# A two-layer decode kernel: V in natural 4 KB runs, exponent on turned scores, one pool of 27 halves, and every K and V load issued as two of 64 partitions

## The chip, the cores and the metric

The kernel runs on one core of a Trainium2 chip. The core has TensorE (PE, matmuls; PEld is its weight load), VectorE (DVE), ScalarE (ACT), GpSimd (POOL) and SyncE (SP, here the only engine that issues transfers), a memory of 128 partitions beside them, and 16 DMA engines that bring data from the large memory. The metric is the device time in microseconds (us), lower is better. The kernel before takes 326.1 us, the median of three runs (323.88 to 326.27).

## The reference

Four tokens, one for each sequence, go twice through an attention block and a feed-forward block; weights and caches are the same both times. Inputs are bfloat16.

```python
# x [4, 1, 448]; k_cache, v_cache [4, 8, 8192, 256]; wq [448, 4096]; wo [4096, 448]
def A(x, k_cache, v_cache, wq, wo):
    W = 2048                                  # min(4096, max(256, 8192 // 4))
    q = (x @ wq).reshape(4, 1, 16, 256).transpose(0, 2, 1, 3)
    k = repeat(k_cache[:, :, 8192 - W:, :], 2, axis=1)   # two query heads to each of 8 K/V heads
    v = repeat(v_cache[:, :, 8192 - W:, :], 2, axis=1)
    p = softmax(einsum("bhqd,bhkd->bhqk", q, k) * 256 ** -0.5)
    o = einsum("bhqk,bhkd->bhqd", p, v)
    return o.transpose(0, 2, 1, 3).reshape(4, 1, 4096) @ wo

def B(x, w_gate, w_up, w_down):               # 448 -> 1792 -> 448
    return (silu(x @ w_gate) * (x @ w_up)) @ w_down

for _ in range(2):
    x = x + A(layernorm(x), k_cache, v_cache, wq, wo)
    x = x + B(layernorm(x), w_gate, w_up, w_down)
```

For one token and one K/V head the last 2048 rows of K and of V are 1 MB each. There are 32 such pairs of token and head, each used in both layers.

## The kernel before

**Work.** The unit is a pair: one token, one layer, one K/V head with its two query heads; there are 64. `steps` lays them out in an order in which token t's first layer runs side by side with token t-1's second layer, shifted by three heads (`SHIFT`), so that the feed-forward block and the next queries of one token are worked out while another token's heads are under way. Of the eight heads of a token five are kept on the chip from the first layer to the second (`KEEP_K`, `KEEP_V`); the other three are loaded twice. So 44 pairs load, and each loads two halves of K and two of V, 512 KB a half.

**A pair** (`pair`, lines 600 to 712). K is loaded in halves in which partition p holds rows 16p to 16p+15, eight of them to a half: one run of 4 KB for each partition (L609). VectorE turns each half in blocks of 32 by 32 into a buffer `KT` (L617), of which there are six, each for a whole K head. GpSimd spreads the queries with a mask (`qe`, L641), so that 32 matmuls (L637) give the scores of all 2048 rows for two query heads in a tile of 128 by 32. VectorE takes the largest of each row (L646), PE spreads it over the partitions (L649), VectorE makes the negated maximum of each query head (L652), and ScalarE the exponents, once for each query head, 128 by 16 (L656). A matmul with a permutation (`permb`, L660) brings the exponents into the order of V's rows, one with ones gives their sums (L663), ScalarE copies them out (`pT`, L666). V is loaded in halves in another order of rows (`(a q g)`), two runs of 2 KB for each partition (L626). Sixteen matmuls multiply with V (L677). The result goes through ScalarE (L689), VectorE (L691), two matmuls (L697) and a multiplication by the inverse sum (L702), which GpSimd works out as a power (L687). `out_proj` multiplies with wo (L724), `residual`, `norm`, `ffn` (L514, L542), `norm` and `qproj` (L473) follow when a token's eight heads are done.

**Buffers.** Fifteen halves (`half`) take all loads of K and V. A half of K is free again after its turn, one of V after its matmuls, or after the second layer's where it is kept. `KT` buffers go round in program order, five of them held for kept heads.

**Order.** Each operation is entered in a graph with an engine, an assumed duration and a rank. `schedule` runs through the graph with an assumed time for every engine and for the DMA channel (`chan`, with `DSTART`, `LAND` and a cost by run length), takes at each moment the waiting operation of lowest rank, and so fixes the order on every engine and the buffer of every load. `_place_waits` then sets the semaphore waits, and `emit` writes the program. SyncE issues the loads in the order found and waits, before each, for the operation that freed its buffer. `KLEAD` and `VLAG` put K's loads 2.2 pairs ahead of their pair and V's 1.3 behind in rank.

Of the kernel before, what the change touches and what calls it, by code (L numbers as in the profile page):

```python
# [6 lines left out]
ALU = mybir.AluOpType  # L7
# [6 lines left out]
B = 4  # L14
# [11 lines left out]
NKT = 6  # L26
NPOOL = 15
# [7 lines left out]
SLEAD = 1.5  # L35
# [8 lines left out]
LAND = 1.5  # L44
DSTART = 2.1
# [10 lines left out]
class Op:  # L56
    __slots__ = ("i", "eng", "dur", "rank", "emit", "deps", "succ", "nbytes", "dsem", "dval",
                 "start", "end", "pos", "waits", "inc", "val", "known", "run", "cell", "rel")

    def __init__(self, i, eng, dur, rank, emit):  # L60
# [7 lines left out]
        self.rel = ()  # L68
        self.inc = False
# [4 lines left out]
class Graph:  # L74
# [12 lines left out]
    def op(self, eng, dur, rank, emit, r=(), w=(), bank=(), acc=()):  # L87

        o = Op(len(self.ops), eng, dur, rank, emit)
        self.ops.append(o)  # L90
# [23 lines left out]
    def dma(self, rank, nbytes, emit, sem, r=(), w=(), run=8192, cell=None):  # L114

        o = self.op(SP, 0.05, rank, emit, r=r, w=w)
        o.run = run
        o.nbytes = nbytes
        o.cell = cell
        if cell is None:  # L120
            self._count(o, sem)
        return o

    def _count(self, o, sem):
        o.dsem = sem
        self.dcount[sem] = self.dcount.get(sem, 0) + 16
        o.dval = self.dcount[sem]


    def schedule(self, npool):  # L130
# [11 lines left out]
        chan = 1.0  # L142
# [3 lines left out]
        while n < len(self.ops):  # L146
            best = None
            for e, lst in avail.items():
                if not lst:
                    continue  # L150
                t = max(free[e], min(ready_at[o] for o in lst))
                if e == SP:
                    first = min((o for o in lst if ready_at[o] <= t + 1e-9), key=lambda o: (o.rank, o.i))
                    if first.cell is not None:
                        if not pool:
                            continue
                        t = max(t, min(pool)[0])
                if best is None or t < best[0]:
                    best = (t, e)
            assert best is not None, "the graph does not complete"  # L160
            t, e = best
            o = min((o for o in avail[e] if ready_at[o] <= t + 1e-9), key=lambda o: (o.rank, o.i))
            if o.cell is not None:
# [4 lines left out]
                self._count(o, f"h{slot[1]}")  # L168
# [4 lines left out]
            free[e] = t + o.dur  # L173
            o.end = t + o.dur
            if o.nbytes:
                chan = max(chan, t + DSTART) + o.nbytes / 16 * (0.007 / o.run + 1 / 26.6e3)
                o.end = chan + LAND - TAIL[SP]
# [50 lines left out]
    def emit(self, eng_name, eng, sems, dsems):  # L228
        for o in self.order[eng_name]:
# [6 lines left out]
            if o.dsem is not None:  # L236
                ins.then_inc(dsems[o.dsem], 16)
# [41 lines left out]
def build(nc, A_x, A_k_cache, A_v_cache, A_wq, A_wo, B_x, B_w_gate, B_w_up, B_w_down, out):  # L279
# [3 lines left out]
    with ExitStack() as es:  # L283
# [9 lines left out]
        KT = [sb(f"KT{s}", [128, 16 * DH], BF16) for s in range(NKT)]  # L293
        identb = sb("identb", [128, 128], BF16)
        permb = sb("permb", [128, 128], BF16)
        onesb = sb("onesb", [128, 128], BF16)
# [526 lines left out]
```

## Time and profile before

| what | value |
|---|---|
| time, median of 3 runs | 326.1 us (323.88 to 326.27) |
| profiled execution, span from the first to the last instruction | 322.9 us |
| mean granted TensorE clock | 1.000 |
| bytes read from the large memory | 104.44 MB, 323 GB/s over the span |
| busy: PE, DVE, ACT, POOL | 232.6, 192.6, 72.4, 84.9 us |
| DMA packets | 42,327, mean 326 GB/s |
| loads of K and of V | 88 each of 512 KB |

The time is that of separate runs; the profile is one execution, of which only the span is known (322.9 us). The page divides the span into 40 slices of about 8.1 us with a digit for the busy tenths of each engine, and names groups of instructions by line and tile. A wait is put down to what ended last. The DMA share is the sum of the times of all packets over the time of 16 engines; it can be a little over 1, where packets of one engine overlap.

### The profile page before, as it was taken

To read this page: it belongs to the slowest core of one execution; us is meant where nothing else is said; L and a number is where in the kernel's file an instruction comes from. 1 tells how busy PE (TensorE), PEld (TensorE's weight loads), DVE (VectorE), ACT (ScalarE), POOL (GpSimd) and SP (SyncE) were. 2 spreads that over 40 slices of the span, in tenths; PEclk is the share of its full clock that TensorE was granted. 3 is DMA by queue.
4 is the path that set the end of the run, shared out by engine and by line. 5 is a ranking of instruction groups with operands and counts; after the bars stand their busy time and mean duration, and the time that the engine had idled before them with its cause. 6 is when DMAs were issued, how large, how long until landed. Compare 5 with 4: busy or idle time off the path is not lost.

```text
span 322.9 us, 12873 instructions
## 1 busy us (share of the span) xinstructions
PE 232.6 (72%) x5728; PEld 169.7 (53%) x5728; DVE 192.6 (60%) x608; ACT 72.4 (22%) x289; POOL 84.9 (26%) x199
## 2 busy tenths in 40 slices
PE   3654454446588788578796895679787959889875
PEld 2542322234476465366664653567555636686554
DVE  5386555652145778765447787855377874656332
ACT  1112111111022333211231322113223322123310
POOL 3312111112023223240233331313233413134221
DMA  7999999999999999999889999999899999748000
GB/s 277 399 407 392 393 396 397 391 396 397 391 362 308 338 368 346 400 362 309 301 272 373 375 351 405 355 365 339 277 359 377 357 386 391 277 140 305 5 0 5
DMA packets 42327, 105.27 MB, mean 326 GB/s; under 512 B 3096, under 2 KB 7200, under 8 KB 41888
## 3 DMA queue, kind: packets, MB, share of 16 engines
q1 hardware_dynamic: 42272, 104.45, 88.0%
q8 instruction: 45, 0.74, 0.9%
q14 instruction: 10, 0.08, 0.1%
HBM read 104.44 MB, written 0.00 MB: 323 GB/s over the span
## 4 chain that ended last, share of the span: by engine, by line
DMA 38%; PE 34%; DVE 12%; SPq 7%; issue 5%; ACT 2%; POOL 0%; DVEq 0%
DMA half<-in_A_k_cache_dram 20%; DMA half<-in_A_v_cache_dram 12%; PE Y L677 11%; PE S L637 8%; DVE KT L617 6%; DMA wd_sb<-in_B_w_down_dram 5%; PE Z L473 4%; SPq L389 4%; PE A L724 3%; PE Z L514 3%; DVE oh L691 2%; PE Z L542 2%; SPq L609 2%; DVE small L652 2%; SPq L626 1%
## 5 line engine op out<-in xcount | busy, mean ns | idle before, releaser
L617 DVE STREAM_TRANSPOSE KT<-half 128x1024 uint32<-128x1024 uint32 x88 | 108.3, 1233 | 13.3 <-DMA half<-in_A_k_cache_dram 12.9
L637 PE MATMUL S<-qe,KT 128*128 128x8 bf16 x2048 | 64.6, 168 | 22.4 <-DVE KT L617 18.5
L677 PE MATMUL Y<-half,pT 128*4 128x256 bf16 x1024 | 70.0, 403 | 9.6 <-DMA half<-in_A_v_cache_dram 8.7
L637 PEld LDWEIGHTS S<-qe,KT 128*128 128x128 bf16 x2048 | 59.7, 104 | 30.7 <-DVE KT L617 20.8
L687 POOL TENSOR_TENSOR small<-small 128x2 f32<-128x2 f32 x64 | 44.3, 696 | 113.5 <-DVE small L669 103.3
L656 ACT ACTIVATE praw<-S,small 128x16 bf16<-128x16 f32 x128 | 28.7, 279 | 84.6 <-DVE small L652 83.9
L691 DVE SCALAR_TENSOR_TENSOR oh<-oh,small,Y 128x256 bf16<-128x256 bf16 x64 | 30.1, 472 | 23.9 <-ACT oh L689 23.4
L689 ACT ACTIVATE oh<-Y 128x256 bf16<-128x256 f32 x64 | 24.6, 384 | 74.2 <-PE Y L677 74.2
L641 POOL TENSOR_TENSOR qe<-qc,qmask 128x64 bf16<-128x64 bf16 x64 | 18.6, 294 | 71.3 <-PE S L637 52.3
L677 PEld LDWEIGHTS Y<-half,pT 128*4 128x4 bf16 x1024 | 20.0, 94 | 21.8 <-DMA half<-in_A_v_cache_dram 11.5
L646 DVE TRANSPOSE_TENSOR_REDUCE pmax<-S 128x1 bf16<-128x32 f32 x64 | 13.4, 211 | 27.1 <-PE S L637 25.3
L724 PE MATMUL A<-oT,wo_sb 128*128 128x1 bf16 (+1 forms) x688 | 24.8, 166 | 6.4 <-DVE oT L702 6.1
L724 PEld LDWEIGHTS A<-oT,wo_sb 128*128 128x128 bf16 x688 | 22.2, 105 | 10.5 <-DVE oT L702 8.5
L697 PE MATMUL Y<-osel,oh 128*128 128x2 bf16 x128 | 13.3, 173 | 17.4 <-DVE oh L691 17.2
L652 DVE TENSOR_REDUCE small<-S 128x2 f32<-128x128 f32 x64 | 17.4, 282 | 10.4 <-PE S L649 8.3
L666 ACT ACTIVATE pT<-Y 128x64 bf16<-128x64 f32 x64 | 14.1, 222 | 40.7 <-PE Y L663 40.4
L697 PEld LDWEIGHTS Y<-osel,oh 128*128 128x128 bf16 x128 | 8.8, 111 | 27.0 <-DVE oh L691 24.5
L649 PE MATMUL S<-identb,pmax 128*128 128x128 bf16 x64 | 16.6, 284 | 4.5 <-DVE pmax L646 3.6
L473 PE MATMUL Z<-xn,wq_sb 128*128 128x1 bf16 (+1 forms) x480 | 15.6, 165 | 2.6 <-DMA wq_sb<-in_A_wq_dram 1.9
L473 PEld LDWEIGHTS Z<-xn,wq_sb 128*128 128x128 bf16 x480 | 14.3, 104 | 3.4 <-DMA wq_sb<-in_A_wq_dram 2.0
L669 DVE TENSOR_REDUCE small<-Y 128x2 f32<-128x32 f32 x64 | 11.0, 177 | 7.1 <-ACT pT L666 6.8
L440 POOL TENSOR_SCALAR st<-st 128x1 f32<-128x1 f32 x16 | 4.3, 267 | 41.2 <-DVE st L428 40.7
(76 smaller groups left out, 212.0 us busy)
## 6 DMA issues: line engine op xcount, KB each, us to landing
half<-in_A_k_cache_dram SPq DMA_DIRECT2D x88, 512.0 KB, 7.0
half<-in_A_v_cache_dram SPq DMA_DIRECT2D x88, 512.0 KB, 6.7
wo_sb<-in_A_wo_dram SPq DMA_DIRECT2D x8, 448.0 KB, 12.3
wq_sb<-in_A_wq_dram SPq DMA_DIRECT2D x3, 1024.0 KB, 6.9
wd_sb<-in_B_w_down_dram SPq DMA_DIRECT2D x1, 1568.0 KB, 16.3
wg_sb<-in_B_w_gate_dram SPq DMA_DIRECT2D x1, 1344.0 KB, 14.2
wu_sb<-in_B_w_up_dram SPq DMA_DIRECT2D x1, 1344.0 KB, 14.7
wq_sb<-in_A_wq_dram SPq DMA_DIRECT2D x1, 512.0 KB, 10.4
```

The costliest lines, as they stand in the source:

```text
L473: last = e.matmul(o, lhsT=lhsT, rhs=rhs, start=(cc == 0 and hh == 0 and ee == 0), stop=(cc == 3), skip_group_check=True)
L617: return e.transpose(dst[:, 2 * hf + q * n:2 * hf + q * n + n], src[:, q * n:q * n + n])
L637: last = e.matmul(Sb[s_][:, 8 * gg:8 * gg + 8], lhsT=kt[:, gg, ce // 2, ce % 2, :], rhs=qe[q_][:, ce, :, :], start=(gg == 0 and ce == 0), ...
L641: g.op(POOL, 0.25, pos - SLEAD - 1, lambda e: e.tensor_tensor(qe[q_][:, :, :, :], qc[t][:, kvh, :, :].unsqueeze(2).broadcast_to([128, 8, 4 ...
L652: g.op(DVE, 0.2, pos, lambda e: e.tensor_reduce(negm[s_][:, :], Sb[s_][:, 128:256].rearrange("p (k n) -> p n k", n=2), AX.X, ALU.max, nega ...
L656: g.op(SCA, 0.17, pos, lambda e, n=n: e.activation(praw[s_][:, :].rearrange("p (k n) -> p n k", n=2)[:, n, :], Sb[s_][:, 0:32].rearrange(" ...
L677: last = e.matmul(Yb[p_][32 * gg:32 * gg + 4, 256:512], lhsT=pT[p_][:, 4 * gg + 2 * hv + a, :, :].rearrange("p y n -> p (y n)"), rhs=half[ ...
L687: g.op(POOL, 0.25, pos, lambda e: e.tensor_tensor(ri[p_][:, :], rs[p_][:, :], expo[:, 1:3], op=ALU.pow), r=(f"rs{p_}", "expo"), w=(f"ri{p_ ...
L689: g.op(SCA, 0.28, pos, lambda e: e.activation(oh[p_][:, :], Yb[p_][:, 256:512], ACT.Copy), r=(f"y{p_}",), w=(f"oh{p_}",), bank=(f"Y{p_}",))
L691: g.op(DVE, 0.4, pos, lambda e: e.scalar_tensor_tensor(out=oh[p_][:, :], in0=oh[p_][:, :], scalar=lomask[:, 0:1], in1=Yb[p_][:, 256:512], ...
L697: last = e.matmul(Yb[p_][:, 2 * dh:2 * dh + 2], lhsT=oh[p_][:, :].rearrange("p (m e) -> p e m", e=2)[:, dh, :], rhs=osel[:, :], start=Fals ...
L724: last = e.matmul(Av[:, cc, sl], lhsT=wo_sb[:, 4 * kvh + k, c0:c0 + 128], rhs=oT[si % 2][:, k % 2, k // 2, 0:n], start=False, stop=False, ...
```

## The change

1. V is loaded as K is: partition p holds rows 16p to 16p+15, in halves of eight rows, one run of 4 KB for each partition.
2. The exponent is taken of turned scores. VectorE turns the tile of scores (128 by 32) in blocks of 32 by 32 into `sM`, and adds a mask that leaves each row in one of four column blocks and puts -1e30 into the others; one exponent over 128 by 128 follows, and one matmul with `fold` brings the result into the order of V's rows. The spread maximum gets -1e30 where a partition's parity belongs to the other query head, by one more matmul (`pbig`) behind the scores. The sums are taken from `pT`. The permutation goes.
3. The six `KT` buffers go; turned K takes halves of the same pool, which now has 27, one for each half of K. A half of turned K is free again after its 16 matmuls. The scores are entered as two operations, one for each half. `schedule` gives out buffers to VectorE's turns too, and SyncE leaves three free for them (`RESERVE`).
4. The plan's constants: a shorter `DSTART` and `LAND`, 0.45 us for each issue on SyncE where 0.05 stood, another cost by run length, and a model of the pages in which PE's instructions are fetched. `SLEAD` goes from 1.5 to 1.0.
5. Every K and V load is issued as two, of partitions 0 to 63 and 64 to 127, both counted on the half's semaphore.
6. Some small tiles share memory: `xio` with `oh`, `t1` with `th`, `xb` with `xn`.

The diff, cut to its core:

```diff
-NKT = 6
-NPOOL = 15
+NPOOL = 27
...
-SLEAD = 1.5
+SLEAD = 1.0
...
-LAND = 1.5
-DSTART = 2.1
+RESERVE = 3
+LAND = 0.45
+DSTART = 1.6
+PAGE, PAGE0 = 128, 85
+FETCH0, FETCH1 = 3.7, 4.4
...
-        o = self.op(SP, 0.05, rank, emit, r=r, w=w)
-        o.run = run
+    def dma(self, rank, nbytes, emit, sem, r=(), w=(), run=8192, cell=None, parts=1):
+
+        o = self.op(SP, 0.45 * parts, rank, emit, r=r, w=w, cell=cell)
+        o.run, o.parts = run, parts
...
-        self.dcount[sem] = self.dcount.get(sem, 0) + 16
+        self.dcount[sem] = self.dcount.get(sem, 0) + 16 * o.parts
...
+                spare = len(pool) > (RESERVE if e == SP else 0)
                 if e == SP:
...
+                    if o.cell is not None:
+                        if not spare:
                             continue
                         t = max(t, min(pool)[0])
...
-                chan = max(chan, t + DSTART) + o.nbytes / 16 * (0.007 / o.run + 1 / 26.6e3)
-                o.end = chan + LAND - TAIL[SP]
+                if t + DSTART > chan:
+                    chan, lag = t + DSTART, 0.0
+                chan += o.nbytes / 16 * (0.009 / o.run + 1 / 27.2e3)
+                o.end = chan + LAND + lag - TAIL[SP]
...
-                ins.then_inc(dsems[o.dsem], 16)
+                for i in ins if o.parts > 1 else (ins,):
+                    i.then_inc(dsems[o.dsem], 16)
...
+        iw = identb[:, :].rearrange("p (u a n) -> p u a n", a=4, n=2)
+        g.op(DVE, 0.2, R0, lambda e: e.tensor_reduce(
+            fold[:, :, :], iw.rearrange("p u a n -> p u n a"), AX.X, ALU.max), r=("identb",), w=("fold",))
+        g.op(DVE, 0.2, R0, lambda e: e.tensor_reduce(
+            amask[:, :], iw.rearrange("p u a n -> p a u n"), AX.XY, ALU.max), r=("identb",), w=("amask",))
+        g.op(DVE, 0.1, R0, lambda e: e.tensor_scalar(
+            amask[:, :], amask[:, :], -1.0, BIG, op0=ALU.add, op1=ALU.mult), r=("amask",), w=("amask",))
...
+            npar[:, :], identb[:, :].rearrange("p (y n) -> p n y", n=2), AX.X, ALU.max), r=("identb",), w=("npar",))
+        g.op(DVE, 0.2, R0, lambda e: e.tensor_scalar(
+            pbig[:, :], npar[:, :], -1.0, BIG, op0=ALU.add, op1=ALU.mult), r=("npar",), w=("pbig",))
...
+            def rows(src, hf):
+                v = src[t, kvh, s0:s0 + WIN, :].rearrange("(p j) d -> p (j d)", p=128)
+                return v[:, 2048 * hf:2048 * hf + 2048]
+
+            if (t, kvh) in k_held:
+                ks, kn = k_held.pop((t, kvh))
+            else:
+                ks, kn = [[], []], kk
+                for hf in range(2):
+                    raw = []
+                    g.dma(pos - KLEAD, 1 << 19, lambda e, raw=raw, hf=hf: [e.dma_start(
+                        half[raw[0]][c:c + 64, :], rows(A_k_cache, hf)[c:c + 64, :]) for c in (0, 64)],
+                        None, w=(f"k{kk}_{hf}",), run=4096, cell=raw, parts=2)
+
+                    def tr(e, raw=raw, hf=hf):
+                        src = half[raw[0]][:, :].bitcast(UINT32).rearrange("p (x k s) -> p x k s", x=4, k=8)
+                        dst = half[ks[hf][0]][:, :].bitcast(UINT32).rearrange("p (k x r) -> p x k r", k=8, x=4)
+                        return e.transpose(dst, src)
+                    g.op(DVE, 1.16, pos, tr, r=(f"k{kk}_{hf}",), w=(f"kt{kk}_{hf}",), cell=ks[hf], rel=(raw,))
+            if (t, kvh) in v_held:
+                vs, vn = v_held.pop((t, kvh))
+            else:
+                vs, vn = [[], []], kk
+                for hv in range(2):
+                    g.dma(pos + VLAG, 1 << 19, lambda e, hv=hv: [e.dma_start(
+                        half[vs[hv][0]][c:c + 64, :], rows(A_v_cache, hv)[c:c + 64, :]) for c in (0, 64)],
+                        None, w=(f"v{kk}_{hv}",), run=4096, cell=vs[hv], parts=2)
+
...
-            g.op(PE, 32 * MM, pos - SLEAD, scores, r=tuple(f"kt{ks}_{hf}_{q}" for hf in range(2) for q in range(TRP)) + (f"qe{q_}",), w=(f"s{s_}",), bank=(f"S{s_}",))
+
+            def scores(e, hf):
+                last = None
+                kt = half[ks[hf][0]][:, :].rearrange("p (g c m v) -> p g c v m", g=2, c=4, v=2)
+                for gg in range(2):
+                    for ce in range(8):
+                        last = e.matmul(Sb[s_][:, 16 * hf + 8 * gg:16 * hf + 8 * gg + 8], lhsT=kt[:, gg, ce // 2, ce % 2, :],
+                                        rhs=qe[q_][:, ce, :, :], start=(hf == 0 and gg == 0 and ce == 0),
+                                        stop=(hf == 1 and gg == 1 and ce == 7), skip_group_check=True)
+                if hf == 1:
+                    last = e.matmul(Sb[s_][:, 128:256], lhsT=identb[:, :], rhs=pbig[:, :].unsqueeze(1).broadcast_to([128, 64, 2]), start=True, stop=False,
+                                    skip_group_check=True)
+                return last
+            for hf in range(2):
+                g.op(PE, (16 + hf) * MM + 0.05 * hf, pos - SLEAD, lambda e, hf=hf: scores(e, hf),
+                     r=(f"kt{kn}_{hf}", f"qe{q_}") + (("identb", "pbig") if hf else ()),
+                     bank=(f"S{s_}",), rel=() if keep_k else (ks[hf],), mm=16 + hf, **(dict(acc=(f"s{s_}",)) if hf else dict(w=(f"s{s_}",))))
...
-            g.op(PE, 0.1, pos, lambda e: e.matmul(
-                Sb[s_][:, 128:256], lhsT=pmax[s_][:, 0:1].broadcast_to([128, 128]), rhs=identb[:, :], start=True, stop=True,
-                skip_group_check=True), r=(f"pmax{s_}", "identb"), w=(f"m{s_}",), bank=(f"S{s_}",))
+            g.op(PE, 0.06, pos, lambda e: e.matmul(
+                Sb[s_][:, 128:256], lhsT=pmax[s_][:, 0:1].broadcast_to([128, 128]), rhs=identb[:, :], start=False, stop=True,
+                skip_group_check=True), r=(f"pmax{s_}", "identb"), w=(f"m{s_}",), bank=(f"S{s_}",), mm=1)
+            g.op(DVE, 0.12, pos, lambda e: e.transpose(sM[s_][:, 3, :], Sb[s_][:, 0:32]), r=(f"s{s_}",), w=("sM",),
+                 bank=(f"S{s_}",))
+            g.op(DVE, 0.19, pos, lambda e: e.tensor_tensor(
+                sM[s_][:, :, :], sM[s_][:, 3, :].unsqueeze(1).broadcast_to([128, 4, 32]),
+                amask[:, :].unsqueeze(2).broadcast_to([128, 4, 32]), op=ALU.add), r=("sM", "amask"), w=("sM",))
             g.op(DVE, 0.2, pos, lambda e: e.tensor_reduce(
-                negm[s_][:, :], Sb[s_][:, 128:256].rearrange("p (k n) -> p n k", n=2), AX.X, ALU.max, negate=True),
+                negm[s_], Sb[s_][:, 128:256], AX.X, ALU.max, negate=True),
                 r=(f"m{s_}",), w=(f"negm{s_}",), bank=(f"S{s_}",))
-            for n in range(2):
-                g.op(SCA, 0.17, pos, lambda e, n=n: e.activation(
-                    praw[s_][:, :].rearrange("p (k n) -> p n k", n=2)[:, n, :],
-                    Sb[s_][:, 0:32].rearrange("p (k n) -> p n k", n=2)[:, n, :], ACT.Exp, bias=negm[s_][:, n:n + 1]),
-                    r=(f"s{s_}", f"negm{s_}"), w=(f"praw{s_}_{n}",), bank=(f"S{s_}",))
-            g.op(PE, 0.03, pos, lambda e: e.matmul(Yb[p_][:, 64:96], lhsT=permb[:, :], rhs=praw[s_][:, :], start=True,
-                                                   stop=False, skip_group_check=True),
-                 r=(f"praw{s_}_0", f"praw{s_}_1", "permb"), w=(f"yp{p_}",), bank=(f"Y{p_}",))
-            g.op(PE, 0.03, pos, lambda e: e.matmul(Yb[p_][:, 32:64], lhsT=onesb[:, :], rhs=praw[s_][:, :], start=False,
-                                                   stop=False, skip_group_check=True),
-                 r=(f"praw{s_}_0", f"praw{s_}_1", "onesb"), w=(f"ysum{p_}",), bank=(f"Y{p_}",))
-            g.op(SCA, 0.13, pos, lambda e: e.activation(
-                pT[p_][:, :, :, :], Yb[p_][:, 64:96].rearrange("p (k n) -> p k n", n=2).unsqueeze(2).broadcast_to(
-                    [128, 16, 2, 2]), ACT.Copy), r=(f"yp{p_}",), w=(f"pT{p_}",), bank=(f"Y{p_}",))
+            g.op(SCA, 0.26, pos, lambda e: e.activation(
+                praw[s_][:, :], sM[s_][:, :, :].rearrange("p a r -> p (a r)"), ACT.Exp, bias=negm[s_]),
+                r=("sM", f"negm{s_}"), w=(f"praw{s_}",))
+            g.op(PE, 0.05, pos, lambda e: e.matmul(
+                Yb[p_][:, 0:32], lhsT=praw[s_][:, :], rhs=fold[:, :, :], start=True, stop=True, skip_group_check=True),
+                r=(f"praw{s_}", "fold"), w=(f"yp{p_}",), bank=(f"Y{p_}",), mm=1)
+            g.op(SCA, 0.15, pos, lambda e: e.activation(
+                pT[p_][:, :, :, :], Yb[p_][:, 0:32].rearrange("p (u n) -> p u n", n=2).unsqueeze(2).broadcast_to(
+                    [128, 16, 2, 2]), ACT.Copy),
+                r=(f"yp{p_}",), w=(f"pT{p_}",), bank=(f"Y{p_}",))
+            g.op(PE, 0.03, pos, lambda e: e.matmul(
+                Yb[p_][:, 32:64], lhsT=onesb[:, 0:1].broadcast_to([128, 128]), rhs=pT[p_][:, :, 0, :], start=False, stop=False, skip_group_check=True),
+                r=(f"pT{p_}", "onesb"), w=(f"ysum{p_}",), bank=(f"Y{p_}",), mm=1)
...
-                for a in range(2):
-                    for gg in range(4):
-                        last = e.matmul(Yb[p_][32 * gg:32 * gg + 4, 256:512],
-                                        lhsT=pT[p_][:, 4 * gg + 2 * hv + a, :, :].rearrange("p y n -> p (y n)"),
-                                        rhs=half[vs[hv][0]][:, 1024 * a + 256 * gg:1024 * a + 256 * gg + 256], start=False, stop=False, skip_group_check=True)
+                for jj in range(8):
+                    u = 4 * (jj // 2) + 2 * hv + jj % 2
+                    gg = jj % 4
+                    last = e.matmul(Yb[p_][32 * gg:32 * gg + 4, 256:512],
+                                    lhsT=pT[p_][:, u, :, :].rearrange("p y n -> p (y n)"),
+                                    rhs=half[vs[hv][0]][:, 256 * jj:256 * jj + 256], start=False, stop=False,
+                                    skip_group_check=True)
                 return last
             for hv in range(2):
...
+                g.op(PE, 0.53, pos, lambda e, hv=hv: pv(e, hv), r=(f"pT{p_}", f"v{vn}_{hv}"), bank=(f"Y{p_}",),
+                     rel=() if keep_v else (vs[hv],), mm=8, **(dict(acc=(f"y{p_}",)) if hv else dict(w=(f"y{p_}",))))
...
```

More of the change, by code (lines that the diff above doesn't have):

```diff
@@ L172, in schedule @@
             o.start = t
-            free[e] = t + o.dur
             o.end = t + o.dur
+            if e == PE:
+                at = t
+                k = done
+                while page < done + o.mm:
+                    at = max(at + o.dur * (page - k) / o.mm, ready)
+                    k = page
+                    page += PAGE
+                    busy = chan > at + 1.0
+                    ready = at + (FETCH1 if busy else FETCH0)
+                    lag = min(lag + busy, 2.0)
+                o.end = at + o.dur * (done + o.mm - k) / o.mm
+                done += o.mm
+            free[e] = o.end
             if o.nbytes:
-                chan = max(chan, t + DSTART) + o.nbytes / 16 * (0.007 / o.run + 1 / 26.6e3)
-                o.end = chan + LAND - TAIL[SP]
+                if t + DSTART > chan:
+                    chan, lag = t + DSTART, 0.0
+                chan += o.nbytes / 16 * (0.009 / o.run + 1 / 27.2e3)
+                o.end = chan + LAND + lag - TAIL[SP]
             o.pos = len(order[e])
@@ L337, in build @@
         R0 = -100.0
+        BIG = 1e30
         MM = 0.0272
```

146 lines of the change are left out of this document (56 added, 90 removed).

## The prediction

> **What bounds the kernel now.** I read the page first: the busy shares, the forty slices, the queue and the chain of waits.
>
> ```profile
> span 322.9 us, 12873 instructions
> ...
> PE 232.6 (72%) x5728; PEld 169.7 (53%) x5728; DVE 192.6 (60%) x608; ACT 72.4 (22%) x289; POOL 84.9 (26%) x199
> ...
> DMA  7999999999999999999889999999899999748000
> GB/s 277 399 407 392 393 396 397 391 396 397 391 362 308 338 368 346 400 362 309 301 272 373 375 351 405 355 365 339 277 359 377 357 386 391 277 140 305 5 0 5
> ...
> q1 hardware_dynamic: 42272, 104.45, 88.0%
> ...
> DMA 38%; PE 34%; DVE 12%; SPq 7%; issue 5%; ACT 2%; POOL 0%; DVEq 0%
> ```
>
> No engine is full, the 16 DMA engines work in nearly every slice until about 299 us, and the chain is shared between loads and TensorE. The next view is the same execution cut into stages (columns: window, its length, busy us and instructions of PE, PEld, DVE, ACT, POOL, then clock, DMA share, GB/s).
>
> ```profile
> 2.00:16.00 14.00, 7.43 (x156) 6.50 (x156) 6.16 (x43) 2.57 (x9) 4.94 (x14) 1.00 0.99 385
> 16.00:96.00 80.00, 44.18 (x1074) 31.29 (x1075) 42.64 (x105) 12.39 (x50) 14.10 (x32) 1.00 1.04 393
> 96.00:128.00 32.00, 26.55 (x643) 18.49 (x639) 22.66 (x62) 9.71 (x40) 9.10 (x20) 1.00 0.95 337
> 128.00:144.00 16.00, 9.73 (x229) 6.92 (x230) 12.04 (x34) 3.40 (x15) 4.94 (x11) 1.00 1.01 382
> 144.00:176.00 32.00, 26.55 (x691) 19.73 (x688) 17.56 (x60) 6.95 (x28) 9.15 (x23) 1.00 0.90 311
> 176.00:208.00 32.00, 23.92 (x547) 16.37 (x545) 25.08 (x66) 9.40 (x39) 8.96 (x18) 1.00 1.01 379
> 208.00:240.00 32.00, 27.04 (x735) 20.70 (x739) 18.39 (x67) 7.44 (x30) 9.20 (x22) 1.00 0.93 327
> 240.00:272.00 32.00, 25.86 (x561) 16.54 (x550) 24.85 (x71) 10.02 (x40) 9.62 (x20) 1.00 1.03 378
> 272.00:299.00 27.00, 24.52 (x700) 20.41 (x697) 15.08 (x58) 5.97 (x25) 9.65 (x26) 1.00 0.73 252
> 299.00:322.90 23.90, 16.83 (x429) 12.74 (x421) 7.19 (x35) 4.50 (x18) 4.45 (x10) 1.00 0.01 3
> ```
>
> Three kinds of stage are to be seen. From 2 to 96 us, and in 128 to 144, 176 to 208 and 240 to 272, the DMA share is 1: loads set the pace. In 96 to 128, 144 to 176, 208 to 240 and 272 to 299 the rate falls to 337, 311, 327 and 252 GB/s while PE is busy 26.5 of 32 us or more: there the loads wait for buffers that PE empties. Against 393 GB/s these four stages lose 32 x (1 - 337/393) = 4.6, 6.7, 5.4 and 9.7 us, together 26 us. After 299 us nothing is loaded.
>
> SyncE's waits agree: its longest are for L677, the matmuls on V that give buffers back.
>
> ```profile
> SPq L609 <- PE Y L677: 25.0, 17, 3.8
> SPq L626 <- PE Y L677: 19.5, 15, 4.0
> ```
>
> For the price of a byte I looked for windows in which a single kind of load runs: 8 KB runs (wq), then 4 KB runs (K), then three windows of 2 KB runs (V).
>
> ```profile
> 3.00:9.00 6.00, 2.77 (x14) 2.27 (x14) 2.92 (x30) 1.28 (x1) 2.91 (x9) 1.00 0.99 414
> 14.00:18.50 4.50, 3.45 (x110) 3.10 (x107) 4.27 (x9) 1.21 (x7) 1.09 (x4) 1.00 1.03 412
> 24.40:25.40 1.00, 0.13 (x3) 0.09 (x1) 1.00 (x4) 0.22 (x1) 0.29 (x1) 1.00 1.02 381
> 30.80:31.90 1.10, 0.15 (x5) 0.04 (x2) 1.10 (x3) 0.22 (x1) 0.04 (x1) 1.00 1.03 382
> 37.40:38.40 1.00, 0.07 (x2) 0.00 (x0) 1.00 (x3) 0.22 (x1) 0.08 (x1) 1.00 1.04 385
> ```
>
> Shared over 16 engines, a 2 KB run takes 2048 x 16 / 383 = 85.6 ns, a 4 KB run 159 ns, an 8 KB run 317 ns. The second 2 KB cost 73.5 ns (27.9 GB/s an engine), the second 4 KB 158 ns (26.0 GB/s). So there is a ceiling of 26 to 28 GB/s for each of 16 ways, whichever tensor is read, and a small cost per run. [...]
>
> **Part 1, V in 4 KB runs.** The page lists the loads:
>
> ```profile
> half<-in_A_k_cache_dram SPq DMA_DIRECT2D x88, 512.0 KB, 7.0
> half<-in_A_v_cache_dram SPq DMA_DIRECT2D x88, 512.0 KB, 6.7
> ...
> wq_sb<-in_A_wq_dram SPq DMA_DIRECT2D x3, 1024.0 KB, 6.9
> ```
>
> V is 88 x 524,288 bytes = 46.1 MB, K the same, together 92.3 MB. V takes 46.1/0.383 = 120.5 us now and 46.1/0.412 = 112.0 us at K's rate: 8.5 us less transfer. It counts only where the share is 1 (14 + 80 + 16 + 32 + 32 = 174 of 297 us): 5.0 us.
>
> **Part 2, exponent on turned scores.** Per pair, against these groups:
>
> ```profile
> L617 DVE STREAM_TRANSPOSE KT<-half 128x1024 uint32<-128x1024 uint32 x88 | 108.3, 1233 | 13.3 <-DMA half<-in_A_k_cache_dram 12.9
> ...
> L691 DVE SCALAR_TENSOR_TENSOR oh<-oh,small,Y 128x256 bf16<-128x256 bf16 x64 | 30.1, 472 | 23.9 <-ACT oh L689 23.4
> ...
> L656 ACT ACTIVATE praw<-S,small 128x16 bf16<-128x16 f32 x128 | 28.7, 279 | 84.6 <-DVE small L652 83.9
> ...
> L689 ACT ACTIVATE oh<-Y 128x256 bf16<-128x256 f32 x64 | 24.6, 384 | 74.2 <-PE Y L677 74.2
> ...
> L646 DVE TRANSPOSE_TENSOR_REDUCE pmax<-S 128x1 bf16<-128x32 f32 x64 | 13.4, 211 | 27.1 <-PE S L637 25.3
> ...
> L652 DVE TENSOR_REDUCE small<-S 128x2 f32<-128x128 f32 x64 | 17.4, 282 | 10.4 <-PE S L649 8.3
> ...
> L649 PE MATMUL S<-identb,pmax 128*128 128x128 bf16 x64 | 16.6, 284 | 4.5 <-DVE pmax L646 3.6
> ...
> L660 PE MATMUL Y<-praw,permb 128*128 128x32 bf16 x64 | 12.6, 199 | 2.8 <-ACT praw L656 2.1
> ```
>
> DVE gains a transpose of 128x32 (0.21 us by L646, same input) and an add over 128x128 (0.28 by L652, same count; up to 0.47 by L691, twice the count): 0.49 us, 31 us over 64 pairs, 192.6 to 224. Both stand between pmax and the negated maximum, while PE makes the broadcast (L649), so perhaps 0.2 us of them lengthens a pair's own chain. ACT loses two exponents of 0.279 and gains one over 128x128 (0.28 to 0.5 us, by L656 and L689): 4 to 18 us less of an engine that is 22% busy. PE loses the permutation (L660), gains the folding matmul of the same width and one of L649's width behind the scores: at most 64 x 0.284 = 18 us. K's transposes (L617) keep their size. That xio, t1 and xb move into memory of other tiles ties only steps that follow one another anyway: nothing. While loads set the pace all of this is free; without that cover, in the stages where DVE has 25 of 32 us, about ten pairs x 0.49 would fill it to 30 of 32. I put that at 4 us, from 0 to 10.
>
> **Part 3, one pool, and the new plan.** 15 halves and six pairs of KT were 27 halves; so many there are now. With five heads kept, 20 are held and 7 stream, and SyncE leaves three free for turned K: four loads in flight. The plan's constants change the order of work on every engine. The price isn't in the rows: at best it gives back the 26 us of the four stages, at worst it loses as much again. Since a half of K now needs a second buffer of the same pool, I take 6 us of gain.
>
> **Part 4, every K and V load as two of 64 partitions.** First the issue:
>
> ```profile
> L609 SPq DMA_DIRECT2D half<-in_A_k_cache_dram x88: 327/388/2530, 3.3 to 279.7; - x88
> ...
> DMA to landing us min/median/max: 4.2/7.0/16.7
> ```
>
> 176 more issues x 0.388 = 68 us on SyncE, 0.78 us for a half that takes 1.27 us to transfer: hidden, SyncE keeps ahead. Queued behind the added issue are only later issues of the same queue; a load that finds the engines empty has its second part 0.39 us later, which counts only where the queue has run dry.
>
> Then the transfer. One bound is nothing: 16 engines still share the load, four partitions each. The other bound is that a ceiling of the landing side holds: partitions 0 to 63 have then half of the places, all 16 engines write to them together, go on together to the other half, and half of the ways stand idle at any time. I take this second bound, since in these windows the share is over 1 (1.03 to 1.04): packets of one engine overlap, so an engine has begun its next packet while the last still lands. An engine that was itself the narrow place couldn't; what is beyond it sets the rate.
>
> The price of that: half of 412 is 206 GB/s; from the steps between run sizes, eight ways at 26.0 to 27.9 give 208 to 223 GB/s. I take 223, as two engines on one way fill the gaps between each other's packets: 92.3/0.223 = 414 us, 2.35 us a half.
>
> [...]
>
> **The sum.** All loads are 104.45 MB; without K and V 12.2 MB, of which wq's three blocks of 1 MB (3.15 MB) at 414 take 7.6 us and the other 9.0 MB at 393, the rate of 16 to 96 us, take 23.0 us. Loads begin at 2 us. The end:
>
> ```profile
> 308.60 1.45 PE L677 MATMUL Y<-half,pT 128*4 128x256 bf16 x24
> ...
> 321.20 0.29 SPq L573 DMA_DIRECT2D out_dram<-KT  x1
> ```
>
> From the last matmuls on V to the end of the span are 14.3 us, which must follow the last landing: 14. So 2 + 7.6 + 23.0 + 414 + 14 = 461 us of span. Nothing else is on the path: PE has at most 251 and DVE 224 us of work, and four loads in flight are 9.4 us of transfer, more than the 4.2 us of the fastest landing and 1.2 us of transpose. The span of before is 3.2 us below the median of 326.1, so 464 us.
>
> **The rivals.** (a) No effect of the split: the ceiling is the engine's, and the first three parts show. 322.9 - 5.0 - 6 + 4 = 316, with 3.2 it is 319 us: faster. It decides once K's 4 KB windows still show over 380 GB/s. For it: nothing in before shows a landing side at all. With the bounds of parts 2 and 3, 303 to 333; DVE filled (part 2 at 10, part 3 at 0) ends this case at 331, slower.
> (b) Staggered engines: fetches and waits set the two engines of one place apart, so that one writes the lower half while the other writes the upper. With a quarter of the time lost instead of half, about 300 GB/s: 308 + 47 + 3 = 358 us (335 to 395). Against it: the buffers make each load wait for its slowest engine, and an engine that ran ahead starts the next load together with the others.
>
> **How the numbers follow.** Halved or nearly: 0.66, 464 us, its own range 395 to 492 (260 GB/s at the fast end, just under 206 with a stall at the slow one). Staggered: 0.12. No effect: 0.22, of which 0.16 faster by over 1%, 0.05 within and 0.01 slower; 1% is about what a measurement of this kernel tells from no change (the three runs of before differ by 0.7%). Slower: 0.66 + 0.12 + 0.01 = 0.79. For 8 in 10 the range must go down into the third case: 318 to 492 leaves out about 0.03 above and 0.12 below.
>
> **What would show it.** Right: the GB/s row near 220 in all slices before the end with the DMA share still near 1, landings of a half well over 7 us, PE near 50% of the span, a chain mostly of K and V loads. Wrong: over 380 GB/s in the first slices (rival a), or 280 to 350 there (b). Part 1 alone shows in (a) as the same rate for K and V; part 2 as about 224 us of DVE and some 60 us of ACT; part 3 as fewer low slices, with SyncE's waits for L677's successor shorter.

## The result

The changed kernel takes 454.85 us, median of four runs (452.62 to 458.25), against 326.09 us before: a ratio of 1.402 (95% interval 1.394 to 1.410; the two medians alone give 1.395). The forecast was 464 us, slower, in a range of 318 to 492 us.

These are lines of the page of the changed kernel, in the order of those shown of before: busy shares, the forty slices (now 11.3 us each), the queue, the chain, and the issues.

```profile
span 453.3 us, 13277 instructions
...
PE 246.1 (54%) x5792; PEld 174.3 (38%) x5792; DVE 210.1 (46%) x740; ACT 69.1 (15%) x225; POOL 85.7 (19%) x199
...
DMA  8999999999998899999999999999999999967800
GB/s 311 244 245 241 239 231 232 231 231 241 384 249 231 205 235 234 236 238 243 255 257 256 254 254 252 249 250 244 248 253 249 252 254 256 253 179 172 201 3 2
...
q1 hardware_dynamic: 33824, 104.46, 94.0%
...
DMA 62%; SPq 14%; PE 13%; DVE 7%; issue 4%; ACT 0%; DVEq 0%
...
half<-in_A_k_cache_dram SPq DMA_DIRECT2D x176, 256.0 KB, 10.6
half<-in_A_v_cache_dram SPq DMA_DIRECT2D x176, 256.0 KB, 9.4
```

The DMA digit is 8 or 9 in each of the first 35 slices (before, 7 to 9), and the bytes are the same (104.46 MB), but from the second slice on they come mostly at 231 to 257 GB/s (205 in the 14th), where before had 391 to 407 while loads set the pace. Only the eleventh slice shows 384: there the feed-forward weights are loaded, most of them with all 128 partitions. PE has little more work (246.1 us for 232.6) and is busy 54% of the span instead of 72%. The chain is 62% loads, where it was 38%.

By stages (columns: window, its length, busy us and instructions of PE, PEld, DVE, ACT, POOL, then clock, DMA share, GB/s):

```profile
16.00:96.00 80.00, 28.97 (x587) 18.02 (x584) 33.88 (x82) 8.37 (x27) 8.69 (x19) 1.00 1.04 236
...
144.00:176.00 32.00, 20.15 (x489) 14.38 (x489) 16.25 (x55) 6.41 (x21) 6.71 (x15) 1.00 0.94 220
176.00:208.00 32.00, 14.00 (x296) 8.94 (x297) 18.55 (x51) 4.33 (x14) 5.13 (x10) 1.00 1.04 237
208.00:240.00 32.00, 21.09 (x571) 16.48 (x573) 14.86 (x55) 5.23 (x17) 6.03 (x15) 1.00 1.03 253
240.00:272.00 32.00, 19.32 (x437) 13.19 (x430) 16.61 (x61) 6.62 (x22) 8.60 (x19) 1.00 1.04 255
272.00:304.00 32.00, 17.05 (x398) 11.96 (x399) 18.86 (x62) 4.86 (x16) 7.47 (x16) 1.00 1.03 250
304.00:336.00 32.00, 20.77 (x541) 15.25 (x538) 14.04 (x51) 5.66 (x19) 5.08 (x13) 1.00 1.00 248
336.00:368.00 32.00, 19.37 (x433) 12.31 (x437) 19.52 (x67) 6.53 (x20) 8.54 (x19) 1.00 1.04 251
368.00:400.00 32.00, 17.94 (x423) 12.18 (x421) 13.97 (x52) 5.32 (x18) 5.36 (x11) 1.00 1.02 252
400.00:432.00 32.00, 23.95 (x619) 18.79 (x623) 17.39 (x70) 6.19 (x21) 9.23 (x22) 1.00 0.70 171
432.00:453.00 21.00, 15.27 (x371) 11.43 (x371) 6.69 (x35) 3.23 (x11) 3.78 (x9) 1.00 0.01 3
```

A share of 1.04 at 236 GB/s is what it means for a load to be slow rather than late: the engines are occupied all the time, and each packet takes them longer: by the trace one of 4 KB took 273 ns at the median, against 159 in the kernel before. No stage shows PE at 26 of 32 us any more.

### The profile page after: what moved, and what is told of

Its sections match the earlier page's. It is cut to its first block, busy times and chain, and to the rows that moved or that the text cites. A ratio compares the mean times of both kernels' runs of the same rounds, so it can differ in the third digit from the quotient of the medians.

```text
span 453.3 us, 13277 instructions
## 1 busy us (share of the span) xinstructions
PE 246.1 (54%) x5792; PEld 174.3 (38%) x5792; DVE 210.1 (46%) x740; ACT 69.1 (15%) x225; POOL 85.7 (19%) x199
## 3 DMA queue, kind: packets, MB, share of 16 engines
q1 hardware_dynamic: 33824, 104.46, 94.0%
## 4 chain that ended last, share of the span: by engine, by line
DMA 62%; SPq 14%; PE 13%; DVE 7%; issue 4%; ACT 0%; DVEq 0%
DMA half<-in_A_v_cache_dram 33%; DMA half<-in_A_k_cache_dram 29%; SPq L656 7%; SPq L670 5%; PE Y L731 4%; DVE half L663 3%; PE S L684 3%; PE A L774 1%; SPq L430 1%; DVE oha L743 1%; PE Z L555 1%; PE Y L749 1%; PE Z L463 1%; PE S L688 0%; PE S L698 0%
## 5 line engine op out<-in xcount | busy, mean ns | idle before, releaser
L663 DVE STREAM_TRANSPOSE half<-half 128x1024 uint32<-128x1024 uint32 x88 | 108.8, 1236 | 112.5 <-DMA half<-in_A_k_cache_dram 112.4
L684 PE MATMUL S<-qe,half 128*128 128x8 bf16 x2048 | 72.4, 169 | 37.0 <-DVE half L663 20.5
L684 PEld LDWEIGHTS S<-qe,half 128*128 128x128 bf16 x2048 | 66.5, 105 | 45.2 <-DVE half L663 21.9
L741 ACT ACTIVATE oha<-Y 128x256 bf16<-128x256 f32 x64 | 24.6, 384 | 154.6 <-PE Y L731 154.3
L709 ACT ACTIVATE praw<-sM,small 128x128 bf16<-128x128 f32 x64 | 25.7, 401 | 130.9 <-DVE sM L703 119.4
L743 DVE SCALAR_TENSOR_TENSOR oha<-oha,small,Y 128x256 bf16<-128x256 bf16 x64 | 29.6, 463 | 15.8 <-ACT oha L741 15.7
L749 PE MATMUL Y<-osel,oha 128*128 128x2 bf16 x128 | 13.3, 173 | 40.5 <-DVE oha L743 38.0
L701 DVE STREAM_TRANSPOSE sM<-S 128x32 f32<-128x32 f32 x64 | 13.3, 207 | 27.1 <-PE S L698 26.7
L514 PEld LDWEIGHTS Z<-xn,wq_sb 128*128 128x128 bf16 x480 | 14.3, 104 | 9.8 <-DVE qc L537 5.3
L703 DVE TENSOR_TENSOR sM<-sM,amask 128x128 f32<-128x128 f32 x64 | 17.9, 280 | 0.1
L688 PE MATMUL S<-pbig,identb 128*128 128x128 bf16 x64 | 17.1, 268 | 0.0
```

The source lines that it names most:

```text
L514: last = e.matmul(o, lhsT=lhsT, rhs=rhs, start=(cc == 0 and hh == 0 and ee == 0), stop=(cc == 3), skip_group_check=True)
L663: return e.transpose(dst, src)
L684: last = e.matmul(Sb[s_][:, 16 * hf + 8 * gg:16 * hf + 8 * gg + 8], lhsT=kt[:, gg, ce // 2, ce % 2, :], rhs=qe[q_][:, ce, :, :], start=(hf ...
L709: g.op(SCA, 0.26, pos, lambda e: e.activation(praw[s_][:, :], sM[s_][:, :, :].rearrange("p a r -> p (a r)"), ACT.Exp, bias=negm[s_]), r=(" ...
L741: g.op(SCA, 0.28, pos, lambda e: e.activation(oh[p_][:, :], Yb[p_][:, 256:512], ACT.Copy), r=(f"y{p_}",), w=(f"oh{p_}",), bank=(f"Y{p_}",))
L743: g.op(DVE, 0.4, pos, lambda e: e.scalar_tensor_tensor(out=oh[p_][:, :], in0=oh[p_][:, :], scalar=lomask[:, 0:1], in1=Yb[p_][:, 256:512], ...
```

## The experiments

The theory is the prediction's: in a load of partitions 0 to 63 or 64 to 127 only half of the places where data land are in use, and these set the rate. It is an assumption: the views show rates, and no places. The rivals: the number or the size of the issues; the other parts of the change; any load of 64 partitions.

**The split undone.** In the changed kernel:

```diff
-lambda e, raw=raw, hf=hf: [e.dma_start(half[raw[0]][c:c + 64, :],
-    rows(A_k_cache, hf)[c:c + 64, :]) for c in (0, 64)], ..., parts=2
+lambda e, raw=raw, hf=hf: e.dma_start(half[raw[0]][:, :], rows(A_k_cache, hf)), ...
```

and the same for V.

> The changed kernel with every K and V load issued as one of 128 partitions again; all else as changed. My theory (the landing side of the loads has half of its places in a load of 64 partitions): K and V run at about 410 GB/s again where loads set the pace, and the time is that of the prediction's third case, about 319 us (303 to 333). Rival A (256 KB loads are too small, or the issues too many): the same, as both are undone here. Rival B (the turned scores, the pool or the new plan cost the time): still over 400 us.

Measured: 322.3 us, 0.986 of before (0.981 to 0.992). Its page:

```profile
GB/s 276 395 410 402 401 405 404 402 404 395 402 318 226 394 401 349 382 295 395 340 334 412 384 379 369 336 310 331 316 412 409 378 338 347 199 186 279 2 2 2
```

In slices 2 to 11 the rate is back at 395 to 410 GB/s, where before had 391 to 407. So the split costs 455 - 322 = 133 us, and the rest of the change is a gain of 1.4%. Rival B falls.

**The split in the other direction**, 128 partitions by half of the columns, so that number and size of the issues stay:

```diff
-half[raw[0]][c:c + 64, :], rows(A_k_cache, hf)[c:c + 64, :]) for c in (0, 64)
+half[raw[0]][:, c:c + 1024], rows(A_k_cache, hf)[:, c:c + 1024]) for c in (0, 1024)
```

> The changed kernel with every K and V load issued as two again, but of all 128 partitions and half of the columns each: the same number of issues and the same 256 KB an issue as changed, runs of 2 KB instead of 4 KB. My theory: all places are reached by each load, so about 383 GB/s as for V before, and the time of e1_whole plus 5 to 12 us. Rival A (number or size of the issues): about 455 us as changed, or more for the shorter runs.

Measured: 333.2 us, 1.020 of before (1.015 to 1.025): 10.9 us more than whole loads, at the upper part of what was expected. Its page:

```profile
GB/s 284 370 393 386 385 385 387 384 388 397 386 322 225 378 384 317 345 309 387 342 329 393 386 382 362 314 318 308 328 391 386 376 349 323 164 156 296 4 2 2
```

With 352 issues of 256 KB slices 3 to 11 still have 384 to 397 GB/s, about the rate of 2 KB runs (381 to 385 in the kernel before). Rival A falls.

**The split alone**, put into the kernel before (V in its 2 KB runs, old pool, old plan): two `dma_start` of `c:c + 64` in both places, 32 counted on the semaphore.

> The kernel before with one part of the change alone: every K and V load as two of 64 partitions; V keeps its 2 KB runs, its pool and its plan. My theory: K and V at 230 to 255 GB/s, 362 to 401 us for 92.3 MB, and with 31 us for the other loads, 2 us ahead and 14 us behind 409 to 448 us of span, 412 to 460 us of time since its buffers stall it a little. Rival B (the other parts cost the time): near 326 us.

Measured: 441.5 us (433.4 to 445.9), 1.355 of before (1.344 to 1.367). That is within what was expected (412 to 460). The split explains the result, in either kernel.

**Loads by themselves.** A kernel of SyncE alone, with stretches of 24 halves on 16 buffers (in short, not the code word for word):

```diff
+phase(lambda d, x: [e.dma_start(d[:, :], x[:, :])])                                        # 1
+phase(lambda d, x: [e.dma_start(d[c:c+64, :], x[c:c+64, :]) for c in (0, 64)])             # 2
+phase(lambda d, x: [e.dma_start(d[:, c:c+1024], x[:, c:c+1024]) for c in (0, 1024)])       # 3
+phase(lambda d, x: [e.dma_start(d[0:64, :], x[0:64, :])])                                  # 4
+phase(lambda d, x: [e.dma_start(d[32:96, :], x[32:96, :])])                                # 5
+phase(lambda d, x: [e.dma_start(d[c:c+32, :], x[c:c+32, :]) for c in (0, 64, 32, 96)])     # 6
```

> Loads alone, nothing is computed and the output is zero. Six stretches, one behind the other, each on the same 16 buffers with 24 loads of K's rows in 4 KB runs (except the third): whole halves of 128 partitions; two of 64 (0 to 63, 64 to 127); two of 128 partitions by 2 KB; partitions 0 to 63 only; partitions 32 to 95 only; four of 32 partitions. [...] Rival A (size and number of the issues): second, third, fourth and fifth alike, near 250, the sixth lower. Rival C (a load of 64 partitions is slow wherever it lies): fourth and fifth alike, near 220, and the third at 383.

The answer by windows, one inside each stretch; the last two columns are the DMA share and GB/s, and the sixth row takes the fifth stretch with its start:

```profile
12.00:31.00 19.00, 0.00 (x0) 0.00 (x0) 1.00 1.03 412
42.00:86.00 44.00, 0.00 (x0) 0.00 (x0) 1.00 1.04 237
104.00:124.00 20.00, 0.00 (x0) 0.00 (x0) 1.00 1.06 387
134.00:156.00 22.00, 0.00 (x0) 0.00 (x0) 1.00 1.04 209
172.00:179.50 7.50, 0.00 (x0) 0.00 (x0) 1.00 1.03 411
162.00:179.50 17.50, 0.00 (x0) 0.00 (x0) 1.00 0.97 350
190.00:228.00 38.00, 0.00 (x0) 0.00 (x0) 1.00 1.02 263
```

The fourth and the fifth row decide. Both are loads of 64 partitions, 256 KB, 4 KB runs, as many of them; only the first partition differs, 0 or 32. The one runs at 209 GB/s, half of 412, the other at 411 once it is under way. It is not that some engines have nothing to do in the fourth: the share, over all 16, is 1.04. The 411 may even be SyncE's: its 24 issues of that stretch take 15.2 us, 0.634 us each, which lets no more than 413 GB/s through. Why the first partition counts, no view shows; that it counts, these two rows do. Rival C falls. In the second row, where the sides change after each load, 237 GB/s are a little over the half: 256 KB take 1.106 us there and 1.254 us in the fourth row. The sixth has 263.

**More orders of loads**, in a second such kernel (again in short):

```diff
+phase: [e.dma_start(d[a:b, :], x[a:b, :]) for a, b in ((32, 96), (0, 32), (96, 128))]   # 1
+phase: [e.dma_start(d[c:128:2, :], x[c:128:2, :]) for c in (0, 1)]                      # 2
+phase: lower of half a, lower of half b, upper of a, upper of b                         # 3
+phase: the lower parts from SyncE, the upper parts from ScalarE                         # 4
```

> Loads alone again, nothing is computed and the output is zero; 16 buffers, 24 halves a stretch, runs of 4 KB. Four stretches: (1) each half as partitions 32 to 95, then 0 to 31, then 96 to 127; (2) as two of 64 partitions, the odd and the even ones; (3) two of 64 partitions, but the lower parts of two halves, then the upper parts of the two; (4) the lower parts issued by SyncE, the upper by ScalarE. In e4_probe 256 KB took 1.106 us where the sides change after each load (237 GB/s), 1.254 us where they never do (209), 0.498 us for 128 KB where they change twice as often (263): 0.13 to 0.15 us are gained at each change. [...] Rival (a load of 64 partitions that isn't 32 to 95 is slow by itself, whatever comes next to it): (3) 237 as with a change after each load.

Windows inside the four stretches:

```profile
20.00:44.00 24.00, 0.00 (x0) 0.00 (x0) 1.00 1.04 285
62.00:80.00 18.00, 0.00 (x0) 0.00 (x0) 1.00 1.03 412
92.00:142.00 50.00, 0.00 (x0) 0.00 (x0) 1.00 1.04 221
160.00:186.00 26.00, 0.00 (x0) 0.00 (x0) 1.00 1.04 295
```

The third is near what follows if all that is gained is gained at each change of sides, 0.148 us by the second and the fourth row of e4_probe: with half as many changes 512 KB take 2.508 - 0.148 = 2.36 us, an estimate, or 222 GB/s, and 221 came, not the rival's 237. That gain is about the time of one run (4 KB took 159 ns in the kernel before). It fits engines that stay in step but for one packet; no view shows the engines one by one. The first, with 32 to 95 in each half, has 285. The second matters most: odd and even partitions, each load again 64 partitions and 256 KB, reach the full rate, 412. From two queues it is 295; why it stops there was not tried, and how the engines share two queues no view shows.

**Odd and even partitions in the kernel.**

```diff
-half[raw[0]][c:c + 64, :], rows(A_k_cache, hf)[c:c + 64, :]) for c in (0, 64)
+half[raw[0]][c:128:2, :], rows(A_k_cache, hf)[c:128:2, :]) for c in (0, 1)
```

> The changed kernel with every K and V load still issued as two of 64 partitions, 256 KB and 4 KB runs, but the even partitions in one and the odd ones in the other, so that each load has all places (e5_probe2: 412 GB/s after a start of some 10 us at 250 to 290). My theory: the time of e1_whole (322.3) plus 0 to 8 us, for the added issues and the slow start after each stretch without loads: 322 to 330 us. Rival (loads of 64 partitions, or twice as many, are slow in this kernel wherever they lie): about 455 us.

Measured: 330.3 us, 1.018 of before (1.012 to 1.025). It is the changed kernel with every load still split in two of 64 partitions, and 124.6 us faster. What it loses against e1_whole, 8 us, is at the upper end of what was expected. The issues on SyncE show a candidate (duration ns min/median/max; first e9_odd_even, then e1_whole):

```profile
L656 SPq DMA_DIRECT2D half<-in_A_k_cache_dram x176: 471/596/1599, 3.2 to 289.1; - x176
```

```profile
L656 SPq DMA_DIRECT2D half<-in_A_k_cache_dram x88: 327/328/2976, 3.2 to 280.3; - x88
```

Two issues of 0.596 us are 1.19 us for a half that needs 1.27 us of transfer, and in e4_probe's fifth stretch, with 0.634 us from issue to issue, two took 1.27 us: SyncE has nothing to spare. The chain of e9_odd_even puts 17% on SyncE, that of e1_whole 8%. That this is the cause of the 8 us was not tried.

**The other parts.** All of these stand on e1_whole. First V alone in 2 KB runs again, as two of 128 partitions by half of the columns:

```diff
-half[vs[hv][0]][:, :], rows(A_v_cache, hv))
+half[vs[hv][0]][:, c:c + 1024], rows(A_v_cache, hv)[:, c:c + 1024]) for c in (0, 1024)
```

> e1_whole with V alone issued as two of 128 partitions and half of the columns, so that V comes in runs of 2 KB again as before the change (with twice the issues), K in runs of 4 KB. By the prediction's part 1, V's 4 KB runs are worth 5.0 us: 327 us. Rival (all of the 8.5 us of transfer count): 331 us. Rival (only issues count, not the runs): 322 us.

Measured: 329.0 us, 1.015 of before (1.009 to 1.021): 6.7 us for V's runs, between the 5.0 of the prediction and the 8.5 of the whole transfer, with 88 more issues and a new plan in it; the two ratios to before set the kernels 9 us apart.

The turn of the scores and the mask made twice (`for _ in range(2):` around both operations):

> e1_whole (loads of 128 partitions) with the turn of the scores and the addition of the mask made twice for each pair: 0.49 us more of VectorE and of the pair's own chain, 31 us over 64 pairs. By the prediction's part 2 the first such 0.49 us cost 4 us (0 to 10), so the second costs as much or somewhat more: 326 to 334 us. If VectorE bounded the stages where it is busy 14 to 15 of 16 us, it would be 335 to 345; if it is all covered, 321 to 324.

Measured: 342.9 us, 1.052 of before (1.042 to 1.061): the second copy costs 20.6 us of its 31, as expected only for the case that VectorE bounds its stages (335 to 345 us). And left out:

```diff
+g.op(DVE, 0.2, R0, lambda e: e.memset(sM[0][:, :, :], 0.0), w=("sM",))
-g.op(DVE, 0.12, pos, lambda e: e.transpose(sM[s_][:, 3, :], Sb[s_][:, 0:32]), ...)
-g.op(DVE, 0.19, pos, lambda e: e.tensor_tensor(sM[s_][:, :, :], ..., op=ALU.add), ...)
```

> e1_whole without the turn of the scores and the addition of the mask (the tile that the exponent reads is set to zero once, so the output isn't the softmax): what part 2 added to VectorE is left out, 0.49 us a pair, and the plan follows. By the prediction's part 2 it gives 4 us (0 to 10): 318 us. By e6_double_turn, where the second copy cost 20 us: 302 to 312 us.

Measured: 324.1 us, 0.995 of before (0.991 to 0.999). Neither expectation held: the first copy costs nothing that shows. Then the addition moved (`g.op(POOL, 0.45, ...)` in place of `g.op(DVE, 0.19, ...)`):

> e1_whole with the addition of the mask on GpSimd, which is busy 27%, instead of VectorE: 0.28 us a pair less there, and two more changes of engine in the pair's chain, with an addition that takes GpSimd some 0.3 to 0.6 us. If VectorE's own time is what e6_double_turn priced (0.63 us of time for each us of work): 322.3 - 64 x 0.28 x 0.63 = 311 us. If it was the length of the pair's chain: 322 to 335 us.

Measured: 321.7 us, 0.990 of before (0.985 to 0.994), the same as e1_whole. GpSimd takes 398 ns for it:

```profile
L703 POOL TENSOR_TENSOR sM<-sM,amask 128x128 f32<-128x128 f32 x64 | 25.5, 398 | 40.8 <-DVE sM L701 39.1
```

That is not the 311 us of a price on VectorE's time, but the lower edge of what was expected for a longer chain (322 to 335): the 18 us that VectorE is spared and the longer chain give nothing and cost nothing that shows. So one copy has room and two have not; whether the second copy's price is VectorE's time or the pair's longer chain isn't shown. A price from doubling doesn't hold for the copy that is there.

The pool, first with one half less kept free (`RESERVE = 2`), then with two halves less (`NPOOL = 25`):

> e1_whole with two instead of three halves kept free from SyncE for turned K, so that one more load can be in flight; the plan follows. By the prediction's part 3 (loads wait for buffers in the four slow stages) it gains 1 to 6 us: 316 to 321 us. Rival (in these stages the loads wait for PE's and VectorE's work itself and another buffer only fills sooner): 321 to 324 us.

> e1_whole with 25 halves in the pool instead of 27; the plan follows. By the prediction's part 3 (loads wait for buffers in four stages) two of some seven free halves less cost much: 330 to 345 us. Rival (the stages are set by the work of PE and VectorE): 321 to 327 us.

Measured: 328.7 us (324.7 to 330.6) for the first, 1.006 of before (1.001 to 1.011), slower than e1_whole by some 6 us (4 by the faster six of its ten runs) where a gain or nothing was expected; 349.3 us for the second, 1.076 (1.071 to 1.081). Two halves less cost 27 us, more than expected (330 to 345 us): the pool is tight. One more load in flight at the price of one buffer for turned K doesn't help. As every such edit makes a new plan, differences of some 6 us between these kernels may be the plan's and not the edit's; and differences of ratios to before come out up to 3 us larger than those of medians.

The fastest kernels are e1_whole and e12_mask_on_gpsimd, at 322 us both 1.0 to 1.4% below before and far below the change.

## Why the prediction was right

**The split (part 4) was the main term, and its price was near the forecast (133 us for 464 - 319 = 145).** That the landing side and not the engine sets the rate was argued from a share over 1 and from half of the places. e4_probe shows the effect with the start partition alone, 209 GB/s from 0 on and 411 from 32 on; places no view shows. The share adds little to that: it is 1.03 at 412 GB/s and 1.04 at 209, much the same at either rate, and no run tested what was inferred from it. Nor does a run show the eight ways behind the sum's 223 GB/s, or two engines that fill each other's gaps on one way: such loads showed 237 by themselves (e4_probe) and 248 to 255 in the kernel from 208 to 400 us. The case with 0.66 came, but its bounds don't follow from their rates: by the prediction's own sum 260 GB/s gives 405 us and not 395, and 206 gives 498 and not 492.

**The sum came out 8 us too high (461 for a span of 453.3), and that it came so near is luck: three errors cancel.** First, the rate of K and V was taken as 223 GB/s. Between 208 and 400 us the windows show 248 to 255, mean 251: 368 us instead of 414. From 16 to 96 us it is lower: 18.9 MB came in 80 us, of which 3.7 MB are wo's (9.4 us at the prediction's 393), so K and V had about 216 GB/s there, an estimate. The bounds of 206 to 223 were meant for engines that stay in step; the stretches of e4_probe and e5_probe2 with nothing else are near them (237 and 221), but whether the engines are in step no view shows. Why the kernel comes to 251 later was not settled; rival (b)'s parting of the engines, by fetches and waits, was not tried, and to its 300 it never came. Second, the end: the last V load lands at about 430 us and the span ends 23 us later, not 14, because other pairs are still to be done. From the last matmuls on V it is 14.3 us, as in the kernel before; but these come 9 us after the last landing, and not at once as the sum has it:

```profile
430.90 0.57 PE L684 MATMUL S<-qe,half 128*128 128x8 bf16 x16
...
438.99 1.45 PE L731 MATMUL Y<-half,pT 128*4 128x256 bf16 x24
...
451.61 0.30 SPq L614 DMA_DIRECT2D out_dram<-oha  x1
```

Third, "nothing else is on the path" was wrong. 453.3 - 2 - 30.6 - 368 - 23 leaves 30 us: some 10 in the slow first stage and 8 before the end, where the share falls to 0.70 as loads wait for buffers that the plan gives to pairs not yet done; the rest in smaller pieces, 4 of them from 144 to 176 us (220 GB/s). So -46, +9 and +30 give the -7.

**Issues on SyncE.** Taken as 0.388 us each and 0.78 us a half; a load of 64 partitions takes 0.597 us at the median and a half 1.19 us. With a half at 2.1 us of transfer there is room for that, and the DMA share is 1.00 to 1.05 in all stages from 16 to 400 us but one (0.94), so it stayed hidden, as said, though with another margin.

**Part 1.** 5.0 us were forecast, 6.7 measured, with the doubts named at e7_v_columns. **Part 2.** VectorE's two operations were priced right (207 and 280 ns for 210 and 282):

```profile
L709 ACT ACTIVATE praw<-sM,small 128x128 bf16<-128x128 f32 x64 | 25.7, 401 | 130.9 <-DVE sM L703 119.4
...
L701 DVE STREAM_TRANSPOSE sM<-S 128x32 f32<-128x32 f32 x64 | 13.3, 207 | 27.1 <-PE S L698 26.7
...
L703 DVE TENSOR_TENSOR sM<-sM,amask 128x128 f32<-128x128 f32 x64 | 17.9, 280 | 0.1
```

Their price was put at 4 us; e10_no_turn shows none. Two of the signs named did not come: VectorE is busy 210 us and not 224, ScalarE 69 and not 60. VectorE's groups add up to 249 us after 219, 30 more as forecast, but records of successive operations overlap, and its busy time, in which no moment counts twice, grew by 17.5. In the same way two exponents one behind the other were busy 28.7 us in all and not 128 x 0.279 = 36, so the exchange spares 3 us where 4 to 18 were forecast. **Part 3.** The gain of 6 us isn't to be seen: 326.1 - 6.7 - 0 would be 319.4, and e1_whole has 322.3. Pool and plan together thus gave nothing or lost about 3 us, which is within what a new plan moves. That the loads of the slow stages wait for buffers was right (e11_pool25), that the new pool eases it was not: the slices of e1_whole still fall to 226, 295 and 310.

**Rival (a)**, 319 us without the split's effect, is e1_whole's 322.3.

## What to carry to other kernels

Ask of each load which partitions it touches, and not only how many: 64 partitions from 32 on, or every second one, load at 411 and 412 GB/s, 64 from 0 on at 209. The other 64 in a load right behind don't make up for it: 237. A full DMA share says that the engines are occupied, not that they are fast (1.04 at 209 GB/s, 1.03 at 412): put GB/s beside it. And the price of doubling a step (20.6 us here) is no price of the step that is there (none that shows).

## What was not expected of the hardware

A split of one load changes what an issue costs SyncE, at the median: 0.328 us for 128 partitions (0.388 in the kernel before), 0.433 us for 128 partitions by half of the columns, 0.597 us for partitions 0 to 63 or 64 to 127, 0.596 us for the even or the odd ones.

Loads of odd and even partitions ran at 294 GB/s in a window of 12 us that begins just after their first issue, before they reached 412, and those of 32 to 95 rose in the same way (350 over the whole stretch, 411 at its end); whole loads had 358 in a window of 6 us near their start. The row of the odd and even loads:

```profile
50.00:62.00 12.00, 0.00 (x0) 0.00 (x0) 1.00 0.90 294
```

Why they rise was not tried. In the kernel with odd and even loads it doesn't show in the stage from 16 to 96 us: both it and e1_whole have 395 GB/s there.

In the profiled execution of e10_no_turn the record has the granted clock of TensorE at half from 113 us on, and nothing slows: from 120 to 160 us PE is busy 30.76 us with 787 matmuls there and 31.47 us with 812 in e1_whole at the full clock, and the execution took 324.1 us, the median of that kernel.

```profile
PEclk9999999999999955555555555555555555555555
```
